# Attention ahead of two MLP layers: scores in one float32 product instead of three, all attention products in quarters of TensorE's array

## The chip, the cores and the metric

The kernel runs on one core of a Trainium2 chip. The metric is the device time of one execution in microseconds (us); lower is better. Engines are named as in the profile: PE is TensorE (products), PEld its weight loads, DVE VectorE, ACT ScalarE, POOL GpSimd, SP the engine whose queue issues most DMAs.

## What is computed

The reference, cut to what matters here (batch 4, 12 heads, 448 tokens, head size 64; two MLP layers follow on 1792 tokens of 768):

```
def _attn_ref(q, k, v):
    scores = scale * np.matmul(q, k.transpose(0, 1, 3, 2)) - np.log(S)
    attn = 1.0 / (1.0 + np.exp(-scores))
    return np.matmul(attn, v).astype(np.float32)
...
x = np.ascontiguousarray(attn_out.transpose(0, 2, 1, 3)).reshape(B * S, H * D)
h = x @ w_in; g = h * np.cos(h); x = g @ w_out
h = x @ w_in; ... ; out = g @ w_out
```

The sigmoid needs no sum over keys, so attention is two products with a sigmoid between. The change touches the attention alone.

## The kernel before

**Attention.** Two heads lie one above the other in the 128 partitions (a pair; 24 pairs, `pairs`). The 448 keys are three chunks of 128 and a half chunk of 64. A *unit* (`units`) is 128 keys of both heads of a pair (`c` = 0, 1, 2), or the 64 last keys of two pairs together (`c` = None): 7 units for two pairs, 84 in all. For each unit `scores` writes the scores (keys in partitions, 448 queries in columns, one bank of PSUM for each head) into one of two buffers of the pool `pss`; ScalarE takes the sigmoid into an SBUF tile `att`; `av` multiplies the values with it and adds up in a bank of the pool `psa` (four banks) over the chunks, with one head in the upper and one in the lower half of the partitions.

For whole chunks the float32 k and q are split into two parts (`prep`: ScalarE copies the high part, VectorE subtracts it to get the low one; type fp32r), and `scores` makes three products (high x high, and the two mixed ones) for each head, with 64 rows and 128 columns of the array. The half chunk is taken from the float32 tiles without a split, as four products of 64 x 64. `av` uses float32: 128 rows and 64 columns for a whole chunk, 64 x 64 for a half. In the trace a float32 product shows as two matmul records and two weight loads. So the array changes between three shapes: 64*128 (`s`), 128*64 (`v`) and 64*64 (`s_None`, and `v` from `a_None`).

**The order.** A loop goes over groups of two units: scores of the group, `slot()`, values of the group before, `slot()` twice. `av_out` (of both pairs when a pair of pairs is complete) copies the sums to SBUF on ScalarE (`ua<-v`) and takes their absolute maximum on VectorE (`mx_x`). Each `slot()` emits the next share of a list `work`: the first layer's weights, which arrive as 64-bit floats (`f1i`, `p1o`), are put together and split by VectorE (lines of `f64_value`, `f64_max`) and ScalarE (`wi`), and at the end of the list x is scaled and split (`xpmax`, `act_scale`, `act_split`). An engine works through its instructions strictly in the order written. `xpmax` has a *gather*: a 128x128 product with the identity (`px_x`) brings a column of maxima into one row, and VectorE reads it (`xm_x`). `pss` and `psa` fill the eight banks of PSUM.

**After attention** the first h tile (`h_matmul`) is computed, then the last two value units, then a second h tile; from there a planner sets the order.

Of the kernel before, what the change touches and what calls it, by code (L numbers as in the profile page):

```python
# [10 lines left out]
F32 = mybir.dt.float32  # L11
# [12 lines left out]
def sigmoid_attention_moe_cos_moe_rational(  # L24
# [17 lines left out]
    P = 128  # L42
# [59 lines left out]

    def ts(eng, o, i, s1, s2=None, op0=ALU.mult, op1=None):
        if s2 is None:
            eng.tensor_scalar(out=o, in0=i, scalar1=s1, scalar2=None, op0=op0)
        else:
            eng.tensor_scalar(out=o, in0=i, scalar1=s1, scalar2=s2, op0=op0, op1=op1)  # L107
# [11 lines left out]
    def xpmax(cols, name, r, place=None):  # L119
# [10 lines left out]
        def gather():  # L130
            ps = (place or PS)("px_" + name)
# [50 lines left out]
    NF64 = [3]  # L182
# [71 lines left out]
    with tc.manual_schedule():  # L254
# [7 lines left out]
        qkv, mqk, att, pvt = {}, {}, {}, {}  # L262

        def load_kq(p):

            bt, hp = pairs[p]
            for nm, src, eng in (("k", k, SY), ("q", q, SY if p else A)):
                pool, tag, n = (wp, "wo", NF) if nm == "k" else (ap_, "rawq", 4)
                t = pool.tile([P, S], F32, tag=tag, name=f"{nm}_{p}", bufs=n)
                eng.dma_start(t, src[bt, 2 * hp:2 * hp + 2].rearrange("h d s -> (h d) s"))  # L270
                qkv[p, nm] = t

        def load_v(o):

            t = ap_.tile([P, v.shape[2]], F32, tag="v", name=f"v_{o}", bufs=2)
            SY.dma_start(t, v[o])
            qkv[o, "v"] = t

        def prep(p):

            steps = {}
            for nm in "kq":
                t = qkv[p, nm]
                hi, lo = (
                    ap_.tile([P, S], F32R, tag=nm + x, name=f"{nm}{x}_{p}", bufs=2) for x in "hl"
                )
                mqk[p, nm] = (hi, lo)
                steps[nm + "h"] = lambda hi=hi, t=t: A.activation(out=hi, in_=t, func=AF.Copy)
                steps[nm + "l"] = lambda hi=hi, lo=lo, t=t: V.tensor_tensor(
                    out=lo, in0=t, in1=hi, op=ALU.subtract  # L290
                )
            return steps

# [5 lines left out]
        def scores(p, c):  # L299

            ps = pss.tile([P, 2, 512], F32, tag="pss", name=f"s_{p}_{c}")
            if c is None:
                for i in range(2):
                    kt, qt = qkv.pop((p + i, "k")), qkv.pop((p + i, "q"))
                    for h in range(2):
                        r, j = slice(h * D, h * D + D), i ^ h
                        T.matmul(ps[j * KH:(j + 1) * KH, h, :S], kt[r, NC * P:S], qt[r], start=True, stop=True)  # L307
            else:
                for i, (kl, ql) in enumerate(((0, 0), (1, 0), (0, 1))):
                    for h in range(2):  # L310
                        r = slice(h * D, h * D + D)
                        T.matmul(  # L312
                            ps[:, h, :S], mqk[p, "k"][kl][r, c * P:c * P + P], mqk[p, "q"][ql][r],
                            start=(i == 0), stop=(i == 2),
                        )
# [4 lines left out]
        def av(p, c):  # L320
            o, i0 = p // 2, p % 2
            vt, at = qkv[o, "v"], att.pop((p, c))
            if i0 == 0 and c == 0:
                for j in range(2):
                    pvt[2 * o + j] = PS(f"v_{2 * o + j}")
            for i in (range(2) if c is None else (i0,)):
                for h in range(2):
                    j = i ^ h
                    if c is None:
                        r, b = slice(j * KH, j * KH + KH), 4 * NC + h  # L330
                    else:
                        r, b = slice(0, P), (2 * j + h) * NC + c
                    T.matmul(  # L333
                        pvt[2 * o + j][h * D:(h + 1) * D, :S], vt[r, b * D:(b + 1) * D], at[r, h],
# [1513 lines left out]
```

## Time and profile before

| | |
|---|---|
| median of 3 runs | 967.65 us (967.36 to 968.49) |
| the profiled execution | 968.57 us, span 966.8 us |
| granted clock, mean | 0.998 |
| busy share of the span | PE 99%, DVE 85%, ACT 64%, POOL 11% |

The span runs from the first to the last instruction; the execution's own time is some 2 us longer. Shares are over the whole span; the attention is its first 15%. A clock of 1.00 is TensorE's 2.4 GHz level.

### The profile page before, as it was taken

To read this page: it belongs to the slowest core of one execution; us is meant where nothing else is said; L and a number is where in the kernel's file an instruction comes from. 1 tells how busy PE (TensorE), PEld (TensorE's weight loads), DVE (VectorE), ACT (ScalarE), POOL (GpSimd) and SP (SyncE) were. 2 spreads that over 40 slices of the span, in tenths; PEclk is the share of its full clock that TensorE was granted. 3 is DMA by queue.
4 is the path that set the end of the run, shared out by engine and by line. 5 is a ranking of instruction groups with operands and counts; after the bars stand their busy time and mean duration, and the time that the engine had idled before them with its cause. 6 is when DMAs were issued, how large, how long until landed. Compare 5 with 4: busy or idle time off the path is not lost.

```text
span 966.8 us, 14097 instructions
## 1 busy us (share of the span) xinstructions
PE 959.6 (99%) x5256; PEld 486.4 (50%) x5256; DVE 823.8 (85%) x1265; ACT 615.0 (64%) x851; POOL 109.9 (11%) x115
## 2 busy tenths in 40 slices
PE   8999999999999999999999999999999999999998
PEld 4444444555555555555555555555555555555554
DVE  6999988999999888969998499878999699999701
ACT  6999986644756445636866567556858567576510
POOL 0000001320122002210134000000220121001000
PEclk9999999999999999999999999999999999999999
DMA  8789883446556676668823115212593356535753
GB/s 316 262 297 306 301 314 132 163 163 230 187 177 205 233 236 209 205 215 261 251 77 115 58 58 179 75 58 68 161 226 123 106 157 178 145 68 147 183 145 104
DMA packets 75286, 171.39 MB, mean 177 GB/s; under 512 B 6481, under 2 KB 48337, under 8 KB 73169
## 3 DMA queue, kind: packets, MB, share of 16 engines
q1 hardware_dynamic: 70608, 163.26, 50.6%
q0 software_dynamic: 4320, 6.88, 4.1%
q8 instruction: 41, 0.67, 0.3%
q10 hardware_dynamic: 288, 0.34, 0.1%
q14 instruction: 29, 0.23, 0.1%
HBM read 129.76 MB, written 33.82 MB: 169 GB/s over the span
## 4 chain that ended last, share of the span: by engine, by line
PE 94%; DVE 4%; ACT 1%; issue 0%; DMA 0%; DVEq 0%; ACTq 0%
PE hx L584 23%; PE o L1013 22%; PE o L1641 17%; PE yw L1445 11%; PE xv L1445 8%; PE v L333 7%; PE s L312 5%; PE s_None L307 1%; DVE ua L110 1%; DVE ua L1576 1%; DVE ba L684 0%; DMA k<-in_k_dram 0%; ACT u L1465 0%; DVE rg L1576 0%; DVE wt L110 0%
## 5 line engine op out<-in xcount | busy, mean ns | idle before, releaser
L1013 PE MATMUL o<-ba,wo 128*128 128x448 f16 x1152 | 226.4, 352 | 0.0
L584 PE MATMUL hx<-ua,wi 128*128 128x448 f16 x1152 | 222.3, 352 | 0.0
L584 PEld LDWEIGHTS <-wi 128*128 128x128 f16 x1152 | 112.4, 98 | 106.1 <-issue 1.4
L1013 PEld LDWEIGHTS <-wo 128*128 128x128 f16 x1152 | 112.6, 98 | 105.0
L1445 PEld LDWEIGHTS <-wi 128*128 128x128 f16 x1008 | 98.6, 98 | 93.6 <-issue 2.0
L1641 PEld LDWEIGHTS <-wt 128*128 128x128 f16 x1008 | 98.6, 98 | 92.0
L1641 PE MATMUL o<-ua,wt 128*128 128x448 f16 x693 | 136.8, 352 | 0.0
L972 POOL TENSOR_TENSOR ba<-ba 128x448 f16<-128x448 f32 x64 | 71.9, 1127 | 448.5 <-DVE ba L107 171.1
L1445 PE MATMUL yw<-ua,wi 128*128 128x448 f16 x576 | 116.8, 352 | 1.0 <-ACT yw L1529 0.6
L1445 PE MATMUL xv<-ua,wi 128*128 128x448 f16 x432 | 87.0, 352 | 0.0
L317 ACT ACTIVATE a<-s,nlogs 128x896 f32<-128x896 f32 x72 | 69.6, 1015 | 8.9 <-PE s L312 8.8
L110 DVE SCALAR_TENSOR_TENSOR w<-w,u 128x896 f32<-128x896 f32 x64 | 69.3, 1086 | 0.6 <-ACT u L1465 0.2
L110 DVE SCALAR_TENSOR_TENSOR ba<-ua,ba 128x768 int32<-128x768 int32 (+1 forms) x68 | 65.7, 971 | 0.2
L333 PE MATMUL v<-a,v 128*64 128x448 f32 x288 | 64.0, 555 | 0.0
L110 DVE SCALAR_TENSOR_TENSOR wt<-o,ig,wt 128x448 f32<-128x448 f32 (+1 forms) x25 | 16.4, 662 | 44.5 <-ACT wt L1678 23.7
L1572 ACT ACTIVATE ua<-ba 128x448 f16<-128x448 f32 x77 | 39.5, 567 | 16.9 <-DVE ba L684 7.5
L1465 ACT ACTIVATE ba<-xv,kp,kp 128x896 f32<-128x896 f32 x16 | 17.5, 1095 | 50.0 <-DVE xv L1536 50.0
L969 ACT ACTIVATE ba<-ba 128x896 f16<-128x896 f32 x32 | 30.4, 949 | 28.1 <-DVE ba L110 27.8
L958 ACT ACTIVATE ba<-ba,halfpi 128x896 f32<-128x896 f32 x32 | 33.3, 1039 | 21.6 <-DVE ba L110 21.3
L110 DVE SCALAR_TENSOR_TENSOR ba<-hx,ck,ba 128x896 f32<-128x896 f32 (+1 forms) x33 | 36.7, 1115 | 8.5 <-ACT ba L951 8.5
L110 DVE SCALAR_TENSOR_TENSOR ba<-ba 128x768 int32<-128x768 int32 (+2 forms) x48 | 40.7, 847 | 3.4 <-DMA wsv<-ba 2.6
L1576 DVE TENSOR_TENSOR ua<-ba,ua 128x448 f16<-128x448 f32 x74 | 42.2, 620 | 1.2 <-ACT ua L1572 1.1
(198 smaller groups left out, 1374.3 us busy)
## 6 DMA issues: line engine op xcount, KB each, us to landing
wi<-wsi SPq DMA_DIRECT2D x16, 1344.0 KB, 5.9
wt<-wso SPq DMA_DIRECT2D x56, 384.0 KB, 3.3
ua<-in_moe_w_out_dram SPq DMA_DIRECT2D x21, 768.0 KB, 4.3
p1o<-in_moe_w_out_dram SPq DMA_DIRECT2D x16, 768.0 KB, 5.8
wsi<-ua SPq DMA_DIRECT2D x42, 256.0 KB, 3.2
f1i<-in_moe_w_in_dram SPq DMA_DIRECT2D x12, 768.0 KB, 5.3
wso<-ba SPq DMA_DIRECT2D x24, 384.0 KB, 2.9
ba<-in_moe_w_out_dram SPq DMA_DIRECT2D x11, 768.0 KB, 4.2
```

Source lines behind the costliest of these rows:

```text
L110: eng.scalar_tensor_tensor(out=o, in0=i0, scalar=s, in1=i1, op0=op0, op1=op1)
L312: T.matmul(ps[:, h, :S], mqk[p, "k"][kl][r, c * P:c * P + P], mqk[p, "q"][ql][r], start=(i == 0), stop=(i == 2),)
L317: A.activation(out=t, in_=ps[:, :, :S], func=AF.Sigmoid, bias=cst["nlogs"], scale=QK)
L333: T.matmul(pvt[2 * o + j][h * D:(h + 1) * D, :S], vt[r, b * D:(b + 1) * D], at[r, h], start=c == (None if i else 0), stop=c == (NC - 1 if ...
L584: T.matmul(ps[:, :S], w[:, wl, f * P:(f + 1) * P], x[:, xl, :], start=(n == 0), stop=(n == 3 * ND - 1),)
L958: A.activation(out=st["r"], in_=st["r"], func=AF.Sin, scale=2.0 * math.pi, bias=cst["halfpi"])
L972: G.tensor_tensor(out=st["g"][:, j, 1, :], in0=st["r"][:, j], in1=st["g"][:, j, 0, :], op=ALU.subtract)
L1013: T.matmul(acc1[bt, e][:, :S], w[:, wl, e * P:(e + 1) * P], g[:, gl, :], start=f == 0 and i == 0, stop=f == NF - 1 and i == 2,)
L1445: T.matmul(o[:, :S], w[:, d, op, wl, :], x[:, xl, :], start=start and n == 0, stop=n == 3 * NDH - 1, skip_group_check=not start,)
L1572: A.activation(out=t[:, 0, :], in_=get(), func=AF.Copy)
L1576: on(l).tensor_tensor(out=t[:, 1, :], in0=get(), in1=t[:, 0, :], op=ALU.subtract)
L1641: T.matmul(o[:, :S], w[:, k % 2, e, wl, :], g[:, gl, :], start=new and i == 0, stop=k == NFH - 1 and i == 2, skip_group_check=op not in FIRST,
```

## The change

- `prep` goes: no splits of k and q. Every product of scores is float32, 64 rows by 64 columns: a unit is four products (two heads by two halves of the 128 keys), each in a quarter of the array.
- `av` takes the 128 keys in two halves of 64, each in a quarter of the array too. Products on different rows of the array write to different banks, so each pair of heads sums in two banks (`pvt[p][0]` and `[1]`), and `av_out` adds them: ScalarE copies one, VectorE adds the other to it and takes the maximum from SBUF.
- All of `psa` is taken by two pairs. The gathers therefore use a buffer of `pss` (`gat`) until the attention ends.
- k and q of a pair share a tile, six tiles in rotation instead of four (q) and a share of 16 (k); three of v instead of two; four buffers for 64-bit weights instead of three. `av_out` runs for a pair as soon as it is complete.
- The last two value units stand before the first h tile.

```diff
+    gat = [PS]
...
         def gather():
-            ps = (place or PS)("px_" + name)
+            ps = (place or gat[-1])("px_" + name)
             T.matmul(ps[:, :P], st.pop(0).bitcast(BF16)[:, 1:2].to_broadcast([P, P]), ident, start=True, stop=True)
             V.tensor_reduce(out=r, in_=ps[:, :P], axis=AX, op=ALU.max)
...
-    NF64 = [3]
+    NF64 = [4]
...
-        qkv, mqk, att, pvt = {}, {}, {}, {}
+        qkv, att, pvt = {}, {}, {}
+        gat.append(lambda name: pss.tile([P, 2, 512], F32, tag="pss", name=name)[:, 0, :])
+        kraw = [halves(view("u", (NU - LENT + 2 * i) * SLOT, 2 * S)) for i in range(3)]
+        kraw += [ap_.tile([P, 2, S], F32, tag=f"kq{i}", name=f"kq{i}") for i in range(3)]
 
         def load_kq(p):
 
-            bt, hp = pairs[p]
-            for nm, src, eng in (("k", k, SY), ("q", q, SY if p else A)):
-                pool, tag, n = (wp, "wo", NF) if nm == "k" else (ap_, "rawq", 4)
-                t = pool.tile([P, S], F32, tag=tag, name=f"{nm}_{p}", bufs=n)
-                eng.dma_start(t, src[bt, 2 * hp:2 * hp + 2].rearrange("h d s -> (h d) s"))
-                qkv[p, nm] = t
+            if p < NP:
+                bt, hp = pairs[p]
+                t = qkv[p] = kraw[p % len(kraw)]
+                for i, (src, eng) in enumerate(((k, SY), (q, SY if p else A))):
+                    eng.dma_start(t[:, i], src[bt, 2 * hp:2 * hp + 2].rearrange("h d s -> (h d) s"))
 
         def load_v(o):
 
-            t = ap_.tile([P, v.shape[2]], F32, tag="v", name=f"v_{o}", bufs=2)
-            SY.dma_start(t, v[o])
-            qkv[o, "v"] = t
-
-        def prep(p):
-
-            steps = {}
-            for nm in "kq":
-                t = qkv[p, nm]
-                hi, lo = (
-                    ap_.tile([P, S], F32R, tag=nm + x, name=f"{nm}{x}_{p}", bufs=2) for x in "hl"
-                )
-                mqk[p, nm] = (hi, lo)
-                steps[nm + "h"] = lambda hi=hi, t=t: A.activation(out=hi, in_=t, func=AF.Copy)
-                steps[nm + "l"] = lambda hi=hi, lo=lo, t=t: V.tensor_tensor(
-                    out=lo, in0=t, in1=hi, op=ALU.subtract
-                )
-            return steps
-
+            if o < NP // 2:
+                t = qkv[o, "v"] = ap_.tile([P, v.shape[2]], F32, tag="v", name=f"v_{o}", bufs=3)
+                SY.dma_start(t, v[o])
...
         def scores(p, c):
 
             ps = pss.tile([P, 2, 512], F32, tag="pss", name=f"s_{p}_{c}")
-            if c is None:
-                for i in range(2):
-                    kt, qt = qkv.pop((p + i, "k")), qkv.pop((p + i, "q"))
-                    for h in range(2):
-                        r, j = slice(h * D, h * D + D), i ^ h
-                        T.matmul(ps[j * KH:(j + 1) * KH, h, :S], kt[r, NC * P:S], qt[r], start=True, stop=True)
-            else:
-                for i, (kl, ql) in enumerate(((0, 0), (1, 0), (0, 1))):
-                    for h in range(2):
-                        r = slice(h * D, h * D + D)
-                        T.matmul(
-                            ps[:, h, :S], mqk[p, "k"][kl][r, c * P:c * P + P], mqk[p, "q"][ql][r],
-                            start=(i == 0), stop=(i == 2),
-                        )
+            for g in range(2):
+                for h in range(2):
+                    r, j = slice(h * D, h * D + D), g ^ h
+                    x, c0 = (qkv[p + j], NC * P) if c is None else (qkv[p], c * P + j * KH)
+                    T.matmul(
+                        ps[j * KH:(j + 1) * KH, h, :S], x[r, 0, c0:c0 + KH], x[r, 1], start=True, stop=True
+                    )
             t = ap_.tile([P, 2, S], F32, tag="att", name=f"a_{p}_{c}", bufs=4)
             A.activation(out=t, in_=ps[:, :, :S], func=AF.Sigmoid, bias=cst["nlogs"], scale=QK)
             att[p, c] = t
         def av(p, c):
             o, i0 = p // 2, p % 2
             vt, at = qkv[o, "v"], att.pop((p, c))
-            if i0 == 0 and c == 0:
-                for j in range(2):
-                    pvt[2 * o + j] = PS(f"v_{2 * o + j}")
-            for i in (range(2) if c is None else (i0,)):
+            for x in (p, p + 1) if c is None else (p,):
+                if x not in pvt:
+                    pvt[x] = [PS(f"v_{x}_{j}") for j in range(2)]
+            for g in range(2):
                 for h in range(2):
-                    j = i ^ h
-                    if c is None:
-                        r, b = slice(j * KH, j * KH + KH), 4 * NC + h
-                    else:
-                        r, b = slice(0, P), (2 * j + h) * NC + c
+                    j = g ^ h
+                    r = slice(j * KH, j * KH + KH)
+                    i, b = (j, 4 * NC + h) if c is None else (i0, (2 * i0 + h) * NC + c)
                     T.matmul(
-                        pvt[2 * o + j][h * D:(h + 1) * D, :S], vt[r, b * D:(b + 1) * D], at[r, h],
-                        start=c == (None if i else 0), stop=c == (NC - 1 if i else None),
+                        pvt[2 * o + i][j][h * D:(h + 1) * D, :S], vt[r, b * D:(b + 1) * D], at[r, h],
+                        start=c == (None if i == j == 1 else 0), stop=c == (None if i == j == 0 else NC - 1),
                     )
 
         def av_out(p):
             bt, hp = pairs[p]
             ps = pvt.pop(p)
             r = U([P, S], F32, f"raw{bt}_{hp}")
-            A.activation(out=r, in_=ps[:, :S], func=AF.Copy)
+            A.activation(out=r, in_=ps[0][:, :S], func=AF.Copy)
+            V.tensor_tensor(out=r, in0=r, in1=ps[1][:, :S], op=ALU.add)
             if hp == 0:
                 mxc[bt] = col(f"mx_x{bt}", ND)
-            V.tensor_reduce(out=mxc[bt][:, hp:hp + 1], in_=ps[:, :S], axis=AX, op=ALU.max, apply_absolute_value=True)
+            V.tensor_reduce(out=mxc[bt][:, hp:hp + 1], in_=r, axis=AX, op=ALU.max, apply_absolute_value=True)
             raw[bt, hp] = r
...
-        steps = prep(0)
-        for st in "kh qh kl ql".split():
-            steps[st]()
         load_kq(2)
         prefetch()
         load_v(1)
-        load_kq(3)
-        prefetch()
-        done = []
+        for p in range(3, len(kraw)):
+            load_kq(p)
+            if p < 5:
+                prefetch()
+        load_v(2)
+
+        def weigh(p, c):
+            av(p, c)
+            if c == (NC - 1 if p % 2 else None):
+                av_out(p)
+                if p % 2:
+                    load_v(p // 2 + 3)
+
         for g in range(0, len(units), 2):
-            due = [1] if g == 0 else []
             for p, c in units[g:g + 2]:
                 scores(p, c)
-                if c is None:
-                    due.append(p + 2)
-                    for x in (p + 4, p + 5):
-                        if x < NP:
-                            load_kq(x)
-                elif p % 2 and c == NC - 1:
-                    due.append(p + 2)
-            low = []
-            for p in due:
-                if p < NP:
-                    steps = prep(p)
-                    steps["kh"]()
-                    steps["qh"]()
-                    low += [steps["kl"], steps["ql"]]
-            for st in low:
-                st()
+                if c == (NC - 1 if p % 2 else None):
+                    load_kq(p + len(kraw))
             slot()
             for p, c in units[g - 2:g] if g else []:
-                av(p, c)
-                if p % 2 and c == NC - 1:
-                    done += [p - 1, p]
-            while done:
-                p = done.pop(0)
-                av_out(p)
-                if p % 2 and p // 2 + 2 < NP // 2:
-                    load_v(p // 2 + 2)
+                weigh(p, c)
             slot()
             slot()
         while work:
...
+        for p, c in units[-2:]:
+            weigh(p, c)
         h0 = h_matmul("x", 0, 0)
         t1_two()
         L1c = {0: l1_consts(0)}
-        for p, c in units[-2:]:
-            av(p, c)
-        av_out(NP - 2)
-        av_out(NP - 1)
         h1 = h_matmul("x", 0, 1)
+        gat.pop()
         pa.close()
```

What the order of instructions becomes, at two places. First TensorE early in the attention, the third group: scores of two units and values of two. `s_` is a buffer of scores, `a_` a sigmoid's result, `v_` ahead of the arrow a bank of sums and behind it the values; in the changed kernel k and q lie in one tile each (`ua`, `kq`). Before:

```order
L312 MATMUL s_0_226<-qh_170,kh_168 128x448 x2
L312 MATMUL s_0_226<-qh_170,kl_169 128x448 x2
L312 MATMUL s_0_226<-ql_171,kh_168 128x448 x2
L312 MATMUL s_1_235<-qh_170,kh_168 128x448 x2
L312 MATMUL s_1_235<-qh_170,kl_169 128x448 x2
L312 MATMUL s_1_235<-ql_171,kh_168 128x448 x2
L333 MATMUL v_216<-a_2_191,v_122 64x448
L333 MATMUL v_217<-a_2_191,v_122 64x448
L333 MATMUL v_216<-a_None,v_122 64x448
L333 MATMUL v_217<-a_None,v_122 64x448 x2
L333 MATMUL v_216<-a_None,v_122 64x448
```

After:

```order
L294 MATMUL s_0_197<-ua 64x448 x4
L294 MATMUL s_1_204<-ua 64x448 x4
L312 MATMUL v_0_183<-a_2_172,v_121 64x448
L312 MATMUL v_1_184<-a_2_172,v_121 64x448 x2
L312 MATMUL v_0_183<-a_2_172,v_121 64x448
L312 MATMUL v_0_183<-a_None,v_121 64x448
L312 MATMUL v_1_216<-a_None,v_121 64x448 x2
L312 MATMUL v_0_183<-a_None,v_121 64x448
```

Each unit is now four float32 products of 64 x 64; the values of a unit go to two banks of its own pair, `v_0` and `v_1`, where before its two heads went to the banks of two pairs (the host laid out the heads of q and k crosswise by fours, `[0, 3, 2, 1]`, and now lays them out in order). The shape 64 x 448 of the output says nothing of the rows used, which are 128 for whole chunks before and 64 after.

Second, the first of the two gathers of x near the end of the attention, on TensorE. Before:

```order
L333 MATMUL v_1387<-a_1_1452,v_1242 64x448
L333 MATMUL v_1386<-a_1_1452,v_1242 64x448
L333 MATMUL v_1387<-a_2_1461,v_1242 64x448
L333 MATMUL v_1386<-a_2_1461,v_1242 64x448
L132 LDWEIGHTS pm_x_1402
L132 MATMUL px_x_1520<-ident,pm_x_1402 128x128
L312 MATMUL s_2_1532<-qh_1430,kh_1428 128x448 x2
L312 MATMUL s_2_1532<-qh_1430,kl_1429 128x448 x2
L312 MATMUL s_2_1532<-ql_1431,kh_1428 128x448 x2
L307 MATMUL s_None<-q_1266,k_1264 64x448 x2
L307 MATMUL s_None<-q_1270,k_1268 64x448 x2
```

After:

```order
L312 MATMUL v_0_1289<-a_1_1275,v_986 64x448
L312 MATMUL v_1_1290<-a_1_1275,v_986 64x448 x2
L312 MATMUL v_0_1289<-a_1_1275,v_986 64x448
L312 MATMUL v_0_1289<-a_2_1282,v_986 64x448
L312 MATMUL v_1_1290<-a_2_1282,v_986 64x448 x2
L312 MATMUL v_0_1289<-a_2_1282,v_986 64x448
L134 LDWEIGHTS pm_x_1241
L134 MATMUL px_x_1337<-ident,pm_x_1241 128x128
L294 MATMUL s_2_1349<-ua 64x448 x4
L294 MATMUL s_None<-ua 64x448
L294 MATMUL s_None<-kq_101 64x448 x2
L294 MATMUL s_None<-ua 64x448
```

It stands at the same place between values and scores. Its buffer is now one of the two of `pss`: `s_2` behind it takes the other, and `s_None` takes the one that the gather held.

VectorE ahead of its read of this gather (`xm_x`). Before:

```order
L144 TENSOR_REDUCE m1o<-p1o_1362 128x1
L110 SCALAR_TENSOR_TENSOR wi_5_1360<-v1i_2_1309,s1i,wi_5_1360 128x512
L345 TENSOR_REDUCE mx_x_1511<-v_1386 128x1
L345 TENSOR_REDUCE mx_x_1511<-v_1387 128x1
L144 TENSOR_REDUCE m1o<-p1o_1397 128x1
L133 TENSOR_REDUCE xm_x_1400<-px_x_1520 128x1
```

After:

```order
L146 TENSOR_REDUCE m1o<-p1o_1183 128x1
L112 SCALAR_TENSOR_TENSOR wi_5_1200<-v1i_2_1148,s1i,wi_5_1200 128x512
L322 TENSOR_TENSOR ua<-ua,v_1_1290 128x448
L325 TENSOR_REDUCE mx_x_1297<-ua 128x1
L146 TENSOR_REDUCE m1o<-p1o_1202 128x1
L135 TENSOR_REDUCE xm_x_1239<-px_x_1337 128x1
```

Ahead of the read there were two maxima out of PSUM and a maximum of weights (`m1o`); now there are the add of the pair just completed, its maximum, and the same `m1o`.

## Rows read from the trace of the kernel before

**Rows 1.** Busy time by stretch: us, PE, PEld, DVE, ACT, POOL, PEclk, DMA share, GB/s.

```profile
5.40:143.60 138.20, 137.59 (x916) 60.69 (x917) 127.58 (x234) 125.81 (x176) 0.00 (x0) 0.99 0.86 307
10.20:131.00 120.80, 120.80 (x814) 53.18 (x812) 116.29 (x213) 111.30 (x156) 0.00 (x0) 1.00 0.87 309
...
143.60:155.00 11.40, 11.40 (x61) 5.47 (x60) 6.93 (x23) 5.86 (x9) 0.00 (x0) 1.00 0.27 80
```

**Rows 2.** Chain that ended last, one cycle: start us, us, what (matmul records).

```profile
22.05 0.91 PE s_None L307 x8
22.96 0.80 PE s L312 x6
...
41.41 1.42 PE s L312 x12
42.83 1.65 PE v L333 x8
44.48 0.91 PE s_None L307 x8
```

**Rows 3.** Timeline of PE and PEld: start us, us, engine, line, names, shape, count.

```profile
33.80 0.14 PEld L333 LDWEIGHTS v<-a,v 128*64 128x64 f32 x2 [0.23 <-issue]
34.17 0.14 PEld L333 LDWEIGHTS v<-a,v 128*64 128x64 f32 x2 [0.23 <-issue]
...
36.45 0.97 PE L333 MATMUL v<-a,v 128*64 128x448 f32 x4
37.35 0.98 PE L333 MATMUL v<-a_None,v 64*64 64x448 f32 x8
...
66.85 0.21 PEld L307 LDWEIGHTS s_None<-q,k 64*64 64x64 f32 x8 [0.70 <-ACT a L317]
66.85 0.98 PE L307 MATMUL s_None<-q,k 64*64 64x448 f32 x8
```

**Rows 4.** Chain that ended last, the start of the program.

```profile
0.74 3.52 DMA k<-in_k_dram
...
10.94 1.74 PE v L333 x8
```

**Rows 5.** Busy time by stretch, the start; columns as in rows 1.

```profile
4.30:7.70 3.40, 1.85 (x13) 1.04 (x12) 1.16 (x2) 2.04 (x4) 0.00 (x0) 1.00 1.00 328
7.70:11.10 3.40, 3.35 (x16) 1.37 (x18) 1.97 (x4) 2.80 (x5) 0.00 (x0) 0.50 0.88 329
11.10:20.00 8.90, 8.90 (x62) 4.37 (x62) 8.43 (x13) 6.73 (x10) 0.00 (x0) 1.00 1.04 405
```

**Rows 6.** Groups by line, 0 to 220 us: busy us, mean ns, idle before.

```profile
L317 ACT ACTIVATE a<-s,nlogs 128x896 f32<-128x896 f32 x72 | 69.6, 1015 | 8.9 <-PE s L312 8.8
...
L289 DVE TENSOR_TENSOR kl<-k,kh 128x448 fp32r<-128x448 f32 x24 | 15.0, 624 | 12.1 <-ACT kh L288 12.0
...
L288 ACT ACTIVATE kh<-k 128x448 fp32r<-128x448 f32 x24 | 14.1, 589 | 1.6 <-DMA k<-in_k_dram 1.6
...
L345 DVE TENSOR_REDUCE mx_x<-v 128x1 f32<-128x448 f32 x24 | 13.8, 617 | 1.1 <-ACT ua L342 1.0
...
L342 ACT ACTIVATE ua<-v 128x448 f32<-128x448 f32 x24 | 11.8, 551 | 5.5 <-PE v L333 5.5
...
L110 DVE SCALAR_TENSOR_TENSOR ba<-hx,kap,ba 128x448 f32<-128x448 f32 x2 | 1.3, 680 | 1.3 <-ACT ba L958 1.3
```

**Rows 7.** Timeline around the first gather of x.

```profile
121.66 0.23 PE L132 MATMUL px_x<-ident,pm_x 128*128 128x128 bf16 x1
...
124.50 0.95 DVE L144 TENSOR_REDUCE m1o<-p1o 128x1 f32<-128x768 f32 x1
...
125.35 0.28 DVE L133 TENSOR_REDUCE xm_x<-px_x 128x1 f32<-128x128 f32 x1
```

**Rows 8.** Chain that ended last, the end of the attention.

```profile
141.94 3.51 PE hx L584 x18
...
145.50 1.65 PE v L333 x8
```

More of the change, by code (lines that the diff above doesn't have):

```diff
@@ L493, in t1_one @@
             st1["m"] = col("xm_t1", tag="xm", bufs=3)
-            spread, st1["g"] = xpmax(
-                i1o, "t1", st1["m"], lambda n: pss.tile([P, 2, 512], F32, tag="pss", name=n)[:, 0, :]
-            )
+            spread, st1["g"] = xpmax(i1o, "t1", st1["m"])
             spread()
@@ L1814, in _lay @@
         b, h, s, d = a.shape
-        a = a.reshape(b, h // 4, 4, s, d)[:, :, [0, 3, 2, 1]].reshape(b, h, s, d).transpose(0, 1, 3, 2)
+        a = a.transpose(0, 1, 3, 2)
     if name == "v":
```

## The prediction

> **What bounds it now.** I first read the busy times by stretch [rows 1]. From the first scores (5.4 us) to the end of the attention work TensorE is busy 137.59 of 138.20 us, VectorE 127.58 and ScalarE 125.81, and behind it (143.6 to 155) TensorE stays full while VectorE falls to 6.93 of 11.40. So TensorE is the bound in the stage that the change touches and in the one after it, with two engines close behind. The chain that ended last agrees: it steps through the attention from one TensorE run to the next [rows 2], and a cycle of four pairs (14 units, 28 products) takes 44.48 - 22.05 = 22.43 us. The order of every engine behind the attention is the same in both kernels, so time that TensorE gains here reaches the end, if no other engine takes over.
>
> The prices of the runs tell more. Two value units in a row take 1.65 us [rows 2]; one alone takes 0.90, from 36.45 to 37.35 [rows 3]. So the second of the same shape costs 0.75, and 0.15 is paid each time the shape of the products changes. For the split scores it is 0.80 for the first unit and 0.62 for the second (1.42 for two) [rows 2]. The weight loads inside a run stand 0.37 us apart (33.80, 34.17), as the rounds of products do, and last 0.14, so they lie under the products [rows 3].
>
> **What the change does, step by step.**
>
> *Products.* Now all 168 products of units (84 scores, 84 values) have one shape, four 64x64 quarters at once. The trace has this shape only alone, between changes: 0.91 us (s_None) [rows 2]. I take 0.75 for one inside a run: 0.91 less the 0.15 of a change, the same 0.75 that the value runs show for float32. Lower bound 0.75 (two rounds 0.37 to 0.375 apart, [rows 3]); upper bound 0.91. Today's cycle holds 12 split scores at 0.62, 12 values and 4 quarter products at 0.75, which is 19.4 us, and 3.0 us of changes of shape. Afterwards it is 28 x 0.75 = 21.0 us without changes: -1.43 in each of six cycles. Scores alone become dearer by 0.13 each; the gain is the changes that go.
>
> *The start.* k lands at 0.74 + 3.52 = 4.26 us [rows 4]. Today its split in ScalarE and VectorE follows, and four units of scores and two of values are done at 10.94 + 1.74 = 12.68. In between the granted clock was 0.50 (the 1.2 GHz level) from 7.7 to 11.1 us, after a stretch in which TensorE was busy 1.85 of 3.40 us [rows 5]. Now the scores start at about 4.4: two units to 5.9; the third waits for the first sigmoid (1.02 us [rows 6], so about 6.4), the fourth for the second and ends at 8.15, the two value units at 9.65. That is -3.0. If the half clock comes again, I lose up to half of 3.4 us: -1.3 is the other bound. The gaps are shorter than before, so I take 9.65.
>
> *The rest.* 80 scores and 82 values at 0.75: 162 x 0.75 = 121.5, to 131.15.
>
> *The two gathers.* The 128x128 gather of an x scale used to take a bank of its own; now it takes one of the two score buffers, and VectorE must read it before the second unit of scores behind it can be written. In the trace the gather ran at 121.66 and VectorE read it at 125.35 + 0.28, 4.0 us later [rows 7]. In the new order VectorE has in front of it, after the end of the pair's last product, the copy by ScalarE (0.55, [rows 6] ua), the new add (0.68), the max (0.62), a max of weights (0.95, [rows 7]) and the read itself (0.28): 3.1 us. TensorE has one unit (0.9 with the change of shape) to put under it. So the first gather stops TensorE for 2.1 us at least and 4.0 - 0.9 = 3.1 at VectorE's present delay: I take 2.5. The second stands behind two units of scores and waits 0.45 for a sigmoid to free its buffer; two value units (1.5) and one of scores follow before its own buffer is wanted, so VectorE's read is covered; without that cover it is another 2.5. The changes of shape cost 2 x (0.16 + 0.16) = 0.64. Together 3.6; for the lower bound I leave the first stop out (1.1), for the upper both gathers stop TensorE for 3.1 (6.8).
>
> *Other engines.* ScalarE loses 48 copies (24 of k, 24 of q, 0.589 each [rows 6]), 28.2 us: 125.8 - 28.2 = 97.6 us. VectorE loses 48 subtractions (0.624 each, 30 us) and gains 24 adds out of PSUM and SBUF. No such add is in the trace; the nearest row with the same operands and shape is 0.680 [rows 6], the max out of PSUM alone 0.617; I take 0.68, or 16.3 us: 114 us. Where two subtractions stand together they overlap by 0.09 us, so less is freed, and 118 is the other bound. Against some 130 us of TensorE it is hidden, but only with 10% to spare, and adds wait on ScalarE's copy. A pair's two banks are wanted again seven products (5.25 us) after its last one; copy and add take 1.2, so VectorE may be 4 us late before TensorE stands. It is latest at the start: its first weights land at about 10 us, and by its order seven operations on weights (some 5.3 us) stand before the first add, which TensorE's products would allow near 13; it is 3 to 4 us late there. I allow 0.65 us for such waits (0 to 3). The moves of k, q and v are as many bytes as before; six buffers for pairs instead of four, and a third for v, only bring them earlier. On SP's queue a load of weights that waits for VectorE holds the loads of k and q behind it; six pairs are 31 us of products, which hide that.
>
> *The end.* The last two value units now stand before the first h tile instead of behind it. Before, they took 1.65 behind 141.94 + 3.51 + 0.06 [rows 8]; the attention's end, with the h tile and gather taken out, is 141.94 + 1.65 = 143.6. The h tile needs the last splits of x; in the new order of VectorE they stand ahead of the adds of the last two pairs, and it has some 13 us to spare over the stage (131 - 118), so I cost this at nothing; without that cover TensorE would stand for the last few of them, 1 to 2 us.
>
> **The sum.** 131.15 + 3.6 + 0.65 = 135.4 against 143.6: -8.2 us. The profiled execution took 968.57 us (span 966.8), so 960.4 for its like; the median of the runs shown is 0.92 lower, which gives 959.5. The case's own range: all best, 131.15 + 1.1 = 132.25, or -11.35 (956.3), and some 0.8 less if the sigmoids at the start hold TensorE less than I took (955.5). Half clock at the start (+1.7), gathers at 6.8 (+3.2) and waits of 3 (+2.35) hardly come all together; the first two make 964.4.
>
> **Rivals.**
>
> *The weight loads are not hidden in quarters: slower.* In a run of quarters the loads of a round go to the rows on which the round before still runs. If they could not overlap, each of two rounds would show its load: the trace's only unit with quarters, 0.91, would then be the price throughout [rows 2], 168 x 0.16 = 27 us more than my sum: 986. It decides from 0.75 + 8.2/168 = 0.80 us a unit. Against it: all eight loads of the lone quarter unit, those of its second round too, lie in the first 0.21 us of 0.98 us of products, and the value runs load the same rows under way [rows 3]. Chance 0.05.
> The Trainium skill states such a rule: on the page "TensorE: Matmul & The Clock Gate", section "Part 3: Packing small matmuls — row/col tiling", weight loads are said to overlap products in flight only where the row groups differ. By that rule this rival would hold, at 986 us or above; the value runs of this trace, all 128 rows in use and 0.37 us between rounds with loads of 0.14 us inside them, do not agree with it.
>
> *VectorE takes over.* If adds cost over a microsecond each with their waits (24 x 0.35 = 8 us more on 118 us) it becomes the bound, TensorE waits for banks at each pair, and most of the gain is gone: 964 to 968. For it: VectorE was busy 116.29 of 120.80 us from 10.2 to 131 [rows 1]. Against it: it frees more than it takes. Chance 0.09.
>
> *Transfers take over: no change.* The stage moves 307 GB/s x 138.2 us = 42.4 MB [rows 1]. If 307 to 309 GB/s is what these queues can do, the stage keeps its length: 967. Against it: from 11.1 to 20 us they moved 405 GB/s [rows 5], and 42.4 MB in 131 us are 324. Chance 0.04.
>
> **Chances.** The forecast 0.82. From no change, this kernel's measurement can tell about 0.2% (1.9 us). Faster: 0.82 and half of the VectorE case, 0.87; the same: the transfers and a part of that case, 0.07; slower: the loads and the worst of VectorE, 0.06. The range from 955.5 to 965.5 leaves out some 0.16: the loads, the transfers and the upper half of VectorE's case.
>
> **What will show it.** In the chain, score and value runs should merge into TensorE steps with 1.50 us for two units and a cycle of 21.0 us; 0.91 a unit would prove the first rival. The first run of values should end near 9.7, with the clock at 1.00 throughout or a half-clock stretch as before. The second unit of scores behind the first gather should start 2 to 3 us late, released by VectorE's read of the gather. The h products should begin near 135. Waits of value products on the add at many pairs, or idle VectorE time ended by transfers of weights, would prove the second or third rival. My number is wrong above all if the gathers or the first 30 us, where VectorE starts late, cost more than I took.

## The result and the profile after

The changed kernel takes 959.92 us (959.47 to 960.20, four runs) against 967.91 us before (967.36 to 968.49, four runs): 0.9917 of the time, 95% interval 0.9900 to 0.9934, or 8.0 us less. The forecast was 959.5 us. The profiled execution took 960.2 us, with a span of 958.4 us.

The head of the page after:

```profile
span 958.4 us, 14810 instructions
...
PE 950.6 (99%) x5688; PEld 505.4 (53%) x5688; DVE 812.9 (85%) x1241; ACT 595.0 (62%) x803; POOL 109.9 (11%) x115
```

The attention by stretch, in the columns of [rows 1]. The last row is the stretch from the first full run of scores to the first gather:

```profile
4.50:136.80 132.30, 130.20 (x1354) 80.11 (x1355) 118.06 (x212) 107.77 (x132) 0.00 (x0) 1.00 0.89 323
...
10.95:113.17 102.22, 102.22 (x1089) 67.93 (x1081) 97.09 (x168) 86.62 (x105) 0.00 (x0) 1.00 0.95 345
```

TensorE is without a gap for 102.22 us and does 136 products of units in them: 0.7516 us each. Transfers moved 345 GB/s there, more than the 307 to 309 of [rows 1]. The chain of waits, in order of time (start, length, what), in four pieces: the start, beside [rows 4]; from 19.97 to 41.01 one cycle of four pairs, beside [rows 2]; the two gathers, beside [rows 7]; and the end of the attention, beside [rows 8]:

```profile
0.74 3.76 DMA ua<-in_q_dram
...
4.54 1.77 PE s L294 x8
...
6.41 1.02 ACT a L298
...
9.44 1.50 PE v L312 x16
10.95 1.50 PE s L294 x16
...
19.97 0.75 PE s_None L294 x8
...
41.01 0.75 PE s_None L294 x8
...
113.17 0.16 PE px_x L134
113.33 0.96 PE s L294 x8
...
114.38 1.02 ACT a L298
...
115.44 1.08 PE s_None L294 x8
...
118.02 0.78 PE s L294 x8
...
118.88 1.02 ACT a L298
...
119.94 0.22 PE px_x L134
120.15 1.66 PE v L312 x16
121.82 1.50 PE s L294 x16
...
132.34 3.01 PE v L312 x32
135.35 3.51 PE hx L547 x18
```

A cycle takes 41.01 - 19.97 = 21.04 us, where it took 22.43. Between 10.95 and 113.17 two units cost 1.50 us whatever they follow: but for the two gathers, no change of shape is paid any more. At each gather TensorE stands for a sigmoid of ScalarE (those at 114.38 and 118.88). How long it stands, by the waits of TensorE (total us, times, longest):

```profile
PE s_None L294 <- ACT a L298: 1.2, 1, 1.2
PE px_x L134 <- ACT a L298: 0.4, 1, 0.4
```

VectorE's read of the first gather, by the timeline:

```profile
116.08 0.28 DVE L135 TENSOR_REDUCE xm_x<-px_x 128x1 f32<-128x128 f32 x1
```

The h products begin at 135.35 us instead of the 143.6 worked out for the kernel before: 8.25 us, and behind it next to nothing is lost or won (the span is 8.4 us shorter). The groups by line, up to 150 us, that answer to [rows 6]:

```profile
L112 DVE SCALAR_TENSOR_TENSOR v1i<-f1i,v1i 128x768 int32<-128x768 int32 (+1 forms) x36 | 31.0, 861 | 0.1
L312 PEld LDWEIGHTS v<-a,v 64*64 64x64 f32 x576 | 34.1, 133 | 20.0 <-issue 3.7 <-ACT a L298 0.5 <-DVE ua L112 0.2
L146 DVE TENSOR_REDUCE m1i<-f1i 128x1 f32<-128x768 f32 (+1 forms) x18 | 15.4, 857 | 0.0
L322 DVE TENSOR_TENSOR ua<-ua,v 128x448 f32<-128x448 f32 x24 | 14.8, 617 | 4.2 <-ACT ua L321 3.9
L109 DVE TENSOR_SCALAR v1i<-f1i 128x768 int32<-128x768 int32 (+1 forms) x18 | 9.2, 509 | 10.1 <-DMA f1i<-in_moe_w_in_dram 10.1
```

The new add takes 0.617 us. VectorE waits for ScalarE's copy 3.9 us in all; in TensorE's list of waits no product of values waits for an add.

### The profile page after: what moved, and what is told of

The parts are those of the page before. It is cut to its first block, busy times and chain, and to the rows that moved or that the text cites. A ratio compares the mean times of both kernels' runs of the same rounds, so it can differ in the third digit from the quotient of the medians.

```text
span 958.4 us, 14810 instructions
## 1 busy us (share of the span) xinstructions
PE 950.6 (99%) x5688; PEld 505.4 (53%) x5688; DVE 812.9 (85%) x1241; ACT 595.0 (62%) x803; POOL 109.9 (11%) x115
## 4 chain that ended last, share of the span: by engine, by line
PE 94%; DVE 3%; ACT 1%; issue 0%; DMA 0%; DVEq 0%; ACTq 0%
PE hx L547 23%; PE o L975 22%; PE o L1603 17%; PE yw L1407 11%; PE xv L1407 8%; PE v L312 7%; PE s L294 6%; DVE ua L112 1%; PE s_None L294 1%; DVE ua L1538 1%; DVE ba L646 0%; DMA ua<-in_q_dram 0%; ACT a L298 0%; ACT u L1427 0%; DVE rg L1538 0%
## 5 line engine op out<-in xcount | busy, mean ns | idle before, releaser
L312 PE MATMUL v<-a,v 64*64 64x448 f32 x576 | 65.1, 536 | 0.0
L312 PEld LDWEIGHTS v<-a,v 64*64 64x64 f32 x576 | 34.1, 133 | 20.0 <-issue 3.7
L913 ACT ACTIVATE ba<-hx,quarter,ck 128x896 int32<-128x896 f32 (+1 forms) x33 | 35.2, 1067 | 13.4 <-PE hx L547 9.1
```

Of the source, the lines that this page charges most:

```text
L312: T.matmul(pvt[2 * o + i][j][h * D:(h + 1) * D, :S], vt[r, b * D:(b + 1) * D], at[r, h], start=c == (None if i == j == 1 else 0), stop=c = ...
L913: A.activation(out=o, in_=x, func=AF.Identity, scale=L1c[bt][0], bias=cst["quarter"])
```

## Experiments

All times are medians, and each kernel is the changed one with the edit shown, unless it says otherwise. The edits are shortened; `...` stands for what is left out. The changed kernel's 959.92 us is what they stand against; the kernel before, run beside them, took 967.6 to 968.1 us.

**One kind of products whole again.** First the values:

```diff
-    for g in range(2): for h in range(2): ... pvt[2 * o + i][j][...], vt[r, ...], at[r, h]
+    for h in range(2): T.matmul(pvt[p][h * D:(h + 1) * D, :S], vt[:, ...], at[:, h], ...)
-    V.tensor_tensor(out=r, in0=r, in1=ps[1][:, :S], op=ALU.add)
```

> Scores stay in quarters; the products of values are whole chunks again (128 rows by 64 columns, one bank per pair, no add on VectorE). The same is computed. Theory (the change gains because all products have one shape, so that the price of a change of shape goes): 14 changes per cycle of four pairs come back, at about 0.155 us each, 6 cycles, so +13 us: near 973 us, above the kernel before, although VectorE loses 24 adds of 0.617 us (14.8 us). Rival (the gain comes from the work that ScalarE and VectorE lost and from the earlier start): 960 us or a little less.

Measured: 972.19 us (ratio to before 1.0044, 1.0032 to 1.0056). Then the scores:

```diff
-    for g in range(2): for h in range(2): ... x[r, 0, c0:c0 + KH], x[r, 1]
+    for h in range(2): T.matmul(ps[:, h, :S], x[r, 0, c * P:c * P + P], x[r, 1], ...)
```

> Values stay in quarters; the float32 products of scores are whole chunks (64 rows by 128 columns for each head, no split). The same is computed. Theory (price of changes of shape): 14 changes per cycle come back, at 0.155 to 0.19 us each, 6 cycles, so +13 to +16 us: 973 to 976 us. Rival (it is enough to drop the split; the shape matters nothing): 960 us.

Measured: 974.05 us (1.0063, 1.0051 to 1.0075). The chain of the first of them, about one change within values (from whole chunks, L319, to quarters, L312), and of the second:

```profile
33.90 1.66 PE s L294 x16
35.56 0.90 PE v L319 x4
36.47 0.91 PE v L312 x8
37.38 1.50 PE s L294 x16
```

```profile
38.06 1.70 PE s L302 x8
39.77 1.66 PE v L318 x16
```

Two units that follow the same shape cost 1.50. After another shape two cost 1.66 and one 0.90 or 0.91; two whole units of scores behind quarters cost 1.70. TensorE is full in both (80.00 of 80.00 us from 20 to 100 us), and VectorE had less to do in the first (61.94 us against 77.08). So +12.3 and +14.1 us come from changes of shape, as the theory has it (14 of them in each of six cycles, half at 0.15 and half at 0.16 us in the first, half at 0.16 and half at 0.20 in the second, are an estimated 13.0 and 15.1 us). The rival, that dropping the split was enough, is out: with only the scores or only the values in quarters, and no split, the kernel is slower than the one before. Both runs keep the rest of the change (more buffers, the order at the end), so the rest alone does not make the gain either. The first run also has a wait at the first gather of x that the changed kernel has not:

```profile
PE s_None L294 <- DVE xm_x L135: 1.3, 1, 1.3
```

**The values in quarters, the split kept.** The kernel before, with the new values and their add. In its first form both pairs' copies and adds came behind the second pair:

```diff
 # in the kernel before
-                        pvt[2 * o + j][h * D:(h + 1) * D, :S], vt[r, b * D:(b + 1) * D], at[r, h],
+                        pvt[2 * o + i][j][h * D:(h + 1) * D, :S], vt[r, b * D:(b + 1) * D], at[r, h],
+            V.tensor_tensor(out=r, in0=r, in1=ps[1][:, :S], op=ALU.add)
```

> The kernel before with one part of the change alone: its values in quarters of the array, in two banks per pair, with the add on VectorE; scores stay split in float32r and whole. The same is computed. On TensorE the changes of shape between scores and values stay, only those between the remainder's values and the others go (2 to 3 per cycle, 6 cycles, 2 to 3 us less). VectorE gets 24 adds of 0.62 us, 15 us on 127.6 of 138.2 us. Theory (the two parts of the change pay only together: alone, this one keeps the changes of shape and makes VectorE the bound): 973 to 980 us. Rival (TensorE still sets the stage and the adds are hidden): 964 to 967 us.

Measured: 982.69 us. There two pairs hold all four banks of values, and in TensorE's list products of values wait 9.0 us for copies. With each pair's sums taken out behind its own last product:

```diff
-                if p % 2 and c == NC - 1:
-                    done += [p - 1, p]
+                if c == (NC - 1 if p % 2 else None):
+                    av_out(p)
...
```

> The kernel before with the values in quarters and the add on VectorE, as in the run before this one, but with a pair's copy, add and maximum issued right behind its last product (there, both pairs' came behind the second, so that two pairs held all four banks of values). The same is computed as in the kernel before. Theory (with the split of k and q kept, VectorE, 15 us of adds on 127.6 of 138.2 us, becomes the bound, and the changes of shape between scores and values stay): 973 to 980 us. Rival (TensorE still sets the stage): 964 to 967 us.

Measured: 977.46 us (1.0103, 1.0087 to 1.0120). Against what the two expectations say, both kernels change what is computed: q and k keep the crosswise layout of the heads, the values do not, so that two heads of each four meet each other's values; the instructions and their sizes are the same. The stretch by windows:

```profile
5.40:153.00 147.60, 141.67 (x1199) 65.32 (x1198) 141.18 (x257) 128.12 (x177) 0.00 (x0) 0.99 0.81 287
```

VectorE is busy 141.18 of 147.60 us here, and from 30 to 62 us the chain runs almost wholly through it. How much of the 9.8 us over the kernel before is VectorE's, and how much a slower stretch of TensorE (its granted clock is 0.89 from 120 to 135 us), is not taken apart. So the parts of the change need each other: the quarters of the values pay only if the scores have their shape too, and with the subtractions left in place the add makes VectorE the bound.

**More and less on VectorE.**

```diff
+            V.tensor_reduce(out=col(f"dm_{p}", ...), in_=r, axis=AX, op=ALU.max, apply_absolute_value=True)
```

> One maximum of 128x448 more on VectorE for each pair, into a column that nothing reads (24 x about 0.53 us = 12.8 us more work; the kernel's own computation is unchanged). VectorE is busy 118 of 132 us in the attention. Theory (TensorE bounds the stage and VectorE has only some 8 to 9 us to spare that it can use): +4 us (2 to 8), 962 to 968 us. Rival (such work lies under TensorE): 0 to +1 us.

```diff
-            V.tensor_reduce(out=mxc[bt][:, hp:hp + 1], in_=r, ...)
+            V.tensor_reduce(out=mxc[bt][:, hp:hp + 1], in_=r[:, :8], ...)
```

> The maximum over a pair's 448 values covers only the first 8 of them (so the scale of x is taken from a part of x; 24 x about 0.45 us = 11 us less on VectorE). Theory (in the changed kernel VectorE is off the path of the attention, but for some tenths in all): 959.3 to 960 us. Rival (VectorE's share of 89% already holds TensorE or the split of x back): 956 us or less.

Measured: 966.41 us with more (+6.5), 960.24 us with less (+0.3, nothing). The attention of the run with less, by windows:

```profile
4.50:136.80 132.30, 130.23 (x1353) 79.84 (x1352) 108.15 (x211) 107.79 (x132) 0.00 (x0) 1.00 0.88 322
```

Taking 10 us off VectorE (108.15 us busy, where it was 118.06) gives nothing; of what was added, 6.5 us come out. The added maxima take 0.61 us each, and VectorE's busy time grows by 11.0 (129.08 us from 4.5 to 143.6) where the expectation had 12.8. So VectorE is off the path, with an estimated 4.5 to 6.3 us to spare (11.0 or 12.8, less 6.5). How a late VectorE reaches TensorE is seen in the run with more, in the timelines of ScalarE and of TensorE (in brackets: idle time, and what ended it):

```profile
109.73 0.94 ACT L361 ACTIVATE wi<-v1i,s1i 128x768 f16<-128x768 f32 x1 [3.36 <-DVE s1i L109]
...
111.00 1.00 ACT L298 ACTIVATE a_None<-s_None,nlogs 128x896 f32<-128x896 f32 x1
```

```profile
112.05 2.78 PE L294 MATMUL s<-ua 64*64 64x448 f32 x16 [1.92 <-ACT a_None L298]
```

A weight's high part waits 3.36 us in ScalarE for a scale from VectorE, the sigmoid stands behind it in ScalarE's order, and scores wait 1.92 us for their buffer; two units then take 2.78 us instead of 1.50, with a granted clock of 0.81 from 109 to 118 us. It is not the banks of values, which the prediction had named as the place.

**The gathers.**

```diff
+    ps = gat[-1](f"ex_{p}"); T.matmul(ps[:, :P], ident[:, 1:2].to_broadcast([P, P]), ident, ...)
+    V.tensor_reduce(out=col(f"em_{p}", ...), in_=ps[:, :P], axis=AX, op=ALU.max)
```

> Eight more 128x128 gathers, one behind each of pairs 2 to 9 of pairs, each read by VectorE into a column that nothing else reads (the kernel's own computation is unchanged). Theory (a gather holds one of the two score buffers, so that TensorE waits for a sigmoid that two buffers would have covered): 1.3 us each with the changes of shape, +10.5 us, near 970 us. Rival (a gather costs only its own product and two changes of shape, 0.32 us each): +2.6 us, 962.5 us.

```diff
-    gat.append(lambda name: pss.tile([P, 2, 512], F32, tag="pss", name=name)[:, 0, :])
+    gat.append(PS)
```

> The gathers of the attention take a bank of the values instead of one of the two score buffers; the same is computed. Theory (in the changed kernel a gather costs 1.0 to 1.2 us beside its two changes of shape, since the score unit behind it finds only one buffer): 2 x 1.1 us come back if a value bank is free when the gather needs it, 957.8 us (957.3 to 958.5). Rival (the stop only moves: the gather or the next pair's first product waits for a bank that VectorE has not read yet): 960 to 962 us.

Measured: 974.79 us with eight more (+14.9), and 957.71 us with gathers in a value bank (957.39 to 957.99; 0.9895 of before, 0.9881 to 0.9908). This one beats both kernels. Its chain, at the start and at the gathers:

```profile
4.39 1.19 PE s L294 x8
...
112.44 0.16 PE px_x L134
112.60 0.91 PE s L294 x8
113.52 0.75 PE s_None L294 x8
...
117.27 0.16 PE px_x L134
117.43 1.67 PE v L312 x16
```

From 112.44 to 119.10 are 6.66 us with eight products of units (6.01): the gathers cost 0.65 us in all, two changes of shape each, and no wait. In the changed kernel they cost 8.65 - 6.01 = 2.64. The hold of a score buffer was worth 1.99 us in the traces, 2.2 in the medians. The run with eight more shows what a hold costs where VectorE's read comes late. Its waits of TensorE (total us, times, longest):

```profile
PE s L294 <- DVE em L522: 6.5, 5, 2.2
PE s_None L294 <- DVE em L522: 3.6, 3, 1.4
```

So TensorE waits for VectorE's reads, and not for a sigmoid, which the expectation had named. These reads stand behind the add and the maximum, and cost 1.3 us each where 1.0 was expected. That is 10.1 us of waits and 8 x 0.32 = 2.6 of changes of shape, less the 1.2 us at the first gather of x, which are not in this list: 11.5 of the 14.9. Behind the longest wait (2.2 us) products ran at the lower level of the clock (1.75 us for a unit and 2.53 for two, instead of 0.98 behind a wait and 1.50; the granted clock is 0.79 from 126 to 134 us), which adds 1.8. The last 1.6 are not taken apart.

**The start.**

```diff
-    WARM = 7
+    WARM = 0
```

> The products that warm TensorE up before the first scores are left out (they feed nothing). Theory (the first score unit of the changed kernel ran at half rate because the clock had not yet risen, although the warming products had run since 1.03 us): without them the clock rises later, some 3.5 us more of the start run at half rate, so +1.5 to +2.5 us: 961.5 to 962.5 us. Rival (the half rate of the first unit has nothing to do with what ran before it): within 0.5 us of 960 us.

Measured: 960.44 us, +0.5. That is the rival's number, though not for its reason. The chain of its start:

```profile
4.19 4.76 PE s L294 x24
8.96 0.93 PE s_None L294 x8
9.88 1.50 PE v L312 x16
```

Three units of scores run in 4.76 us, 1.59 each, all at half rate, where the changed kernel had one such unit. So the warming products do bring the full rate forward: the last unit at half rate ends at 8.95 us, not at 6.31, or by 7.35 in the run with less on VectorE, whose start is the same as the changed kernel's and whose first two units took 2.97 us. But a unit at half rate takes not much longer than the sigmoids and waits that pace these units anyway, and up to the end of the first values only 0.43 us are lost (11.38 against 10.95); counted from the first scores, which start 0.35 us earlier here, it is 0.78.

**A cheaper score product.** From the third pair on, float16 halves of k and q made by GpSimd, then the same for four pairs only, with the gathers in a value bank. To make room, k and q have four and five tiles in rotation instead of six; that is not tested apart:

```diff
+    G.tensor_copy(out=hi[:, i], in_=t[:, i])
+    G.tensor_tensor(out=lo[:, i], in0=t[:, i], in1=hi[:, i], op=ALU.subtract)
+    for n, (kl, ql) in enumerate(((0, 0), (1, 0), (0, 1))): ... # float16, four quarters each
```

> From the third pair on, k and q are split into float16 halves by GpSimd and the scores are three products of halves, in quarters like the values; the product of the two low halves is left out, as it was in the kernel before. Three rounds of four quarters at one pass should take 0.56 to 0.62 us a unit instead of 0.75, 77 units: 10 to 14 us less on TensorE. Theory (VectorE is the next bound, with some 6 us to spare by the run with one more maximum): 953 to 955 us. First rival (TensorE alone sets the stage): 946 to 950 us. Second rival (three times as many weight loads in short rounds are no longer hidden, or GpSimd's work slows VectorE): 958 us or more.

> Gathers in a value bank, and four of the 24 pairs with scores from float16 halves that GpSimd splits (without the product of the two low halves); all else as in the changed kernel. By the run with all pairs split, a unit costs 0.57 instead of 0.75 us (4 pairs, 14 units: -2.5 us on TensorE) and a split pair costs VectorE about 0.9 us beside GpSimd (+3.7 us, with some 4 us to spare). Theory (both add up): 955 to 956 us. Rival (the stretches beside GpSimd hold TensorE back at once): 957.7 us or more.

Measured: 975.9 us (+16.0), and 959.21 us for four pairs, 1.5 above the best. On TensorE the idea holds: the chain of the first has

```profile
140.27 1.14 PE s L308 x24
```

0.57 us for a unit of scores. It has 12 weight loads where the float32 unit has 8 (not three times as many, as the expectation says), and they stay hidden. But VectorE slows down beside GpSimd. Its groups by line from 20 to 140 us:

```profile
L112 DVE SCALAR_TENSOR_TENSOR v1i<-f1i,v1i 128x768 int32<-128x768 int32 (+1 forms) x32 | 34.3, 1072 | 0.1
L112 DVE SCALAR_TENSOR_TENSOR wi<-v1i,s1i,wi 128x768 f16<-128x768 f32 (+1 forms) x18 | 22.2, 1236 | 0.0
L109 DVE TENSOR_SCALAR v1i<-f1i 128x768 int32<-128x768 int32 (+1 forms) x15 | 14.0, 934 | 0.0
L146 DVE TENSOR_REDUCE m1i<-f1i 128x1 f32<-128x768 f32 (+1 forms) x16 | 13.7, 859 | 0.0
```

Against 861, 922, 509 and 857 ns, that is 32 x 0.21 + 18 x 0.31 + 15 x 0.43 = 18.7 us more. Less the 4.5 to 6.3 to spare this makes 12 to 14 of the 16.0 us; the rest I have not taken apart. Here products of values do wait for adds, 9.7 us in TensorE's list: the wait that the prediction's second rival names. With four pairs split, products of scores wait for sigmoids behind VectorE's late results, 2.1 us behind the start, and the 2.5 us gained on TensorE are given back with 1.5 more; what makes up the rest of these 4.0 is not shown. That the two effects would only add up was wrong.

## Why the prediction held, step by step

The forecast of 959.5 us was right within 0.4 us, and the sum's total was nearly exact (135.4 us forecast, 135.35 in the trace). Three of its terms were off, one up and two down, and nearly cancel.

- *Products at 0.75, none at a change of shape.* Right: 0.7516, cycle 21.04 against 21.0. The first rival (0.91) is out. Weight loads of 0.133 us lie inside these 0.75. The Trainium skill, page "TensorE: Matmul & The Clock Gate", section "Part 3: Packing small matmuls — row/col tiling", has a sentence that lets loads overlap only with products on other rows; this trace does not agree with it, as each load of a second round goes to rows that are in use. The same section also lets a load into a background weight buffer go ahead, and by that the loads here could be hidden. The price of a change of shape, on which the whole gain rests, is shown by both runs with one kind of products whole. The same skill says on the page "TensorEngine Tiling (Array Packing)", section "Key Properties", that a change of tiling mode drains TensorE. The runs agree in that each change costs time, 0.15 to 0.20 us; a drain itself is in no view.
- *The start.* Forecast 9.65 us, measured 10.95: mis-sized by 1.3. The scores had to wait for q, which landed at 4.50 us, 0.24 later than the 4.26 taken from k, and the first unit of scores took 1.77 us instead of 0.75, so that the sigmoids that pace the next units all began a microsecond late. I had allowed for a half rate, but behind 7.7 us, where [rows 5] showed it; in the new kernel the clock reads 1.00 there, and it lay at the very first unit. How much of that unit it takes varies from one execution to the next: with the gathers in a value bank, whose start is the same, it took 1.19 us.
- *The gathers.* Forecast 3.6, measured 2.64. The stop of the first gather was mis-sized, 1.2 us instead of 2.5, and the wait that was to end it was the wrong one for this kernel. In the chain `s_None` follows the sigmoid of the unit before it (114.38 + 1.02) and starts at 115.44, ahead of VectorE's read (116.08 to 116.36). So it cannot have the gather's buffer, as the text on the order of instructions and the prediction have it; it takes the buffer of `s_2`, which that sigmoid must free first. The gather holds the other one until 116.4, and the unit that wants it comes at 118.02: the read stopped nothing. Which buffer `s_None` gets is settled where the program is built, and it is not the same in all runs. With whole values, and with less on VectorE, `s_None` at this same gather waits for VectorE's read, as forecast, 1.3 and 1.5 us. So the wait I had in mind exists, and also behind eight more gathers, but it too is shorter than 2.5. The second gather waits 0.4 us for a sigmoid, as forecast (0.45). All in all 2.0 us are waits and restarts, and 0.64 changes of shape.
- *Waits on the add, 0.65.* Measured: nothing. What is left, 135.35 - 10.95 - 121.5 - 2.64 = 0.26, is the price of a unit, 0.7516 instead of 0.75, times 162. The term was put in without a row that shows such a wait, and no product of values waits for an add. The add cost 0.617, not 0.68.
- *The rival VectorE.* Rightly judged near: an estimated 4.5 to 6.3 us to spare, by the run with more. VectorE was busy 118.06 us, which is the prediction's other bound and not its 114. ScalarE was busy 107.77 us and not 97.6: its busy time fell by 18.0 us and not by the 28.2 of 48 copies. Neither sets the stage. The rival transfers is out (345 GB/s, TensorE full).
- *The end at nothing.* Right: the h products follow the last values at once.

So the mechanism of the gain was right, the changes of shape that go. The start (+1.30), the gathers (-0.96), the waits (-0.65) and the price of a unit (+0.26) almost cancel, and the closeness of the total is chance. Without the hold of a score buffer the change gives 10.2 us (957.71).

## What to carry to other kernels

Price the changes of shape in TensorE's order along with its products: here 3.0 us of them in a cycle outweighed 12 scores dearer by 0.13 us each, but only once all products had the one shape. VectorE had no room for the add until the subtractions went, so both belong into one change. A scratch product should take its place in the pool with most slack: here in the pool of four banks, not in the pool of two, where it cost 2 us. And a forecast of a wait for a buffer needs to know which buffer the program gets.

## What the runs showed of the hardware that was not expected

- The granted clock reads 1.00 from 4.54 to 6.10 us although the first unit of scores takes 1.77 us, over twice what one takes later; without the warming products the column still reads 1.00 from 4.19 to 8.90 us while three units run at half rate. At the start of these programs the durations tell the rate, not the column.
- GpSimd slows some operations of VectorE by 0.2 to 0.4 us each and leaves others as they are: those with two inputs from SBUF (861 to 1072 ns) and the fast one with one (509 to 934, where a maximum over as many elements takes 857) suffer, the maxima (857 and 859) and the add with an input from PSUM (617 and 610) do not. In the run with four pairs the first of them (128x768 alone) takes 0.96 us from 40 to 75 us, where GpSimd rests, and 1.39 beside it from 76 to 87 (two of them). The Trainium skill, page "SBUF — State Buffer", section "🔬 SBUF: two separate sides", tells of a port pair that the two engines lock against each other, taken by VectorE's operations with two SBUF inputs or in a faster mode. The rows agree for all the operations named.
